# A fused RWKV attention and cosine feed-forward kernel: chunks taken in the order of time over all four batches, with a new hand-written first order

## The chip, the cores and the metric

The kernel runs on one core of a Trainium2 chip. The metric is the device time of one execution in microseconds (us), the median of several runs. Five engines work beside each other: TensorE (PE, its weight loads shown as PEld), VectorE (DVE), ScalarE (ACT), GpSimd (POOL), and SyncE (SP), which here only issues transfers. Each engine runs its own list of instructions in order; semaphores tie the lists together.

## The reference

For each batch and head a 48x48 state runs along 768 steps; the output of all heads is then put through a feed-forward layer with the gate h·cos(h).

```python
batch, n_heads, seq, head_dim = (4, 8, 768, 48)
for t in range(S):
    cur = einsum('bhd,bhe->bhde', u * k[t], v[t])
    y[:, :, t] = einsum('bhd,bhde->bhe', r[t], state + cur)
    state = w[t][..., None] * state + einsum('bhd,bhe->bhde', k[t], v[t])
x = y.transpose(0, 2, 1, 3).reshape(3072, 384)
h = x @ w_in                      # 384 x 2048
out = (h * cos(h)) @ w_out        # 2048 x 384
```

## The kernel before

The time axis is cut into chunks of C=128 steps, so there are 6 chunks for each of 4 batches, 24 in all. Two chunks are worked on together as one **block** (`BLK`=2, i.e. 256 rows of x), so there are 12 blocks. Block i holds chunks number 2i and 2i+1 of the list `order`. Before the change the list takes batches 0 and 1 from their first to their last chunk and then batches 2 and 3: blocks 0 to 5 are a chain through the state of the first two batches, blocks 6 to 11 one through that of the others.

The attention of chunk j is cut into steps, each a short function. `load` fetches the tile `tt` with r, k and w transposed. `decay` (DVE) makes the running products of w by two scans (L207, L213) with `wholes` and a reciprocal (L211, L212) between them, and scales r (L217) and k (L218, on POOL at first) in place. `diag` makes the diagonal of the score matrix: for the first six chunks with PE (`rkt` L204 on DVE, `pc` L224 on PE, `cd` on ACT), later with DVE from a second layout `rk` (L229, L230, L232); POOL spreads it into `asb` (L236). `a` makes the scores (`pa` L259) and copies them into `asb` (DVE, L261). `t` turns k (`pt` L268, copied to `kn`), `d` scales the old state (`dd` L249, copied into `past`). Steps of a whole block are `s` (new state, `pst` L286, `sn` L291/L293), `o` (own part of the output, `py` L314/L319) and `p` (part from the past state, L329/L333, then `xT`: a high part by ACT and a low part by DVE, L144). Chunks with c=0 have no past state: no `d`, and a `p` without matmuls.

The feed-forward of a block is 8 **units** of 256 hidden columns. `mm1` of a unit is 18 matmuls into one PSUM bank `ph` (L381). The **gate** follows: ACT (L357), DVE (L358), ACT sine (L359), DVE product (L360, which also frees the bank), ACT high part `gs` (L141), two POOL low parts (L144). `mm2` is 12 matmuls (L397) into two accumulator banks. All weights stay in SBUF, but each of the 16 slices must be made first from a packed form `raw`: three ACT passes (L163, L166, L167), DVE L168, L169, an ACT cast, and a DVE difference (`w<-h,w`, L144). `raw` slots are a ring of five (`RING`), so a `raw` load waits for ACT's L167 of the slice five before it.

The order in which PE and SP take the first part is written out by hand in `START` (words as `a2` = scores of chunk 2; `f` = fetch a slice, `w` = make one); `PAIR` says for which of blocks 0 and 1 each of the first 16 units is. After that `PLAN` repeats eight slots per block. PE keeps the written order; in the first part SP's transfers keep it too. DVE, ACT and POOL are ordered by the framework's scheduler. A step that isn't there yet when it's needed is called in by `att()` with its `NEEDS` and the rules on buffers. PSUM has eight banks: three for attention (a0 to a2), three for `ph` (h0 to h2), two accumulators; while blocks 0 and 1 run side by side a2 and h2 serve as block 1's accumulators, and attention and `ph` have two banks each.

Of the kernel before, what the change touches and what calls it, by code (L numbers as in the profile page):

```python
# [26 lines left out]
NCB = 6  # L27
W129 = NP * 129
BLK = 2
# [4 lines left out]
RING = 5  # L34
BY_HAND = "P"
MERGE = 1
BUFS = dict(tt=4, rk=2, v=4, h=2, rd=1, rr=7, gs=2, asb=4, ahl=2, sn=2, past=2, xT=2, kn=2, ee=2, dd=2, cd=1, rkt=1)
LEAST = 1e-15
W_SCALE = 2.0 ** 8
INV2PI = 1.0 / (2.0 * math.pi)  # L40
BANKS = dict(a=("a0", "a1", "a2"), h=("h0", "h1", "h2"))
PAIR_W = 2 * HD + 16
VW = NP * PAIR_W
PASSES = ((0, 0), (0, 1), (1, 0))
# [13 lines left out]
        "mm1 mm2",  # L58
        "mm1 mm2",
        "mm1 d+4 d+5 mm2 decay+5 lr+6"]  # L60
START = ["lv0 decay0 diag0 t0 load0 f load1 f d0 a0 f f diag1 w t1 decay2 o0 w a1 f diag2 d1 x0 f load3 p0 f",
# [4 lines left out]
PAIR = "0001100111101010"  # L66
NEEDS = dict(decay="load", lr="load", lv="load", diag="lr", d="decay", a="decay diag", t="decay",
             o="a lv", s="t d lv", p="o d")

# [2 lines left out]
def rwkv_cos_ffn(ctx: ExitStack, tc: tile.TileContext, tr, tn, tv, u, ut, wts, w, rkw, vst, us, xs, out):  # L72
# [15 lines left out]

    def bank(kind, shape, name):

        tags = dict(a=("a0", "a1"), h=("h0", "h1")) if paired[0] else BANKS
        turn[kind] += 1
        return ps.tile(shape, F32, tag=tags[kind][turn[kind] % len(tags[kind])], name=name)

    paired = [True]

    def buf(tag, shape, dtype, name=None, pool=sb):
        return pool.tile(shape, dtype, tag=tag, name=name or tag, bufs=BUFS.get(tag, 1))
    ident = cst.tile([C, C], F32, name="ident")
# [22 lines left out]
    past = [cst.tile([R, NP, R96], F32, name="past%d" % n) for n in range(BLK)]  # L122
# [49 lines left out]
            low_part("wlo%d" % kind, rest, hf, high)  # L172

    NB = NG // NCB
    order = [(b0 + bb) * NCB + c for b0 in range(0, NB, BLK) for c in range(NCB) for bb in range(BLK)]
    atts, states, outs, xts, units, accs = {}, {}, {}, {}, {}, {}

    def att_load(j):
        a = atts[j] = {"j": j}
        a["g"] = g = order[j]  # L180
        a["b"], a["c"] = divmod(g, NCB)
        a["tt"] = tt = buf("tt", [R, TRW], F32)
        for cols in ((1024, TRW), (512, 1024), (0, 512)) if j < IN_PARTS else ((0, TRW),):
            E["qt"].dma_start(out=tt[:, slice(*cols)], in_=tr[g, :, slice(*cols)])
        a["r3"] = tt[:, 0:512].rearrange("p (a t) -> p a t", a=NP)
        a["k3"] = tt[:, 512:1024].rearrange("p (a t) -> p a t", a=NP)
        if j == 0:
            E["qt"].dma_start(out=u_by_head, in_=ut)
        if j == BY_PE:
            E["qt"].dma_start(out=u_sb, in_=u.to_broadcast([C, DM]))  # L190
# [178 lines left out]
    def mm1(t):  # L369
        i, u = seq[t]  # L370
        weights("f", (u + 1) * FU + LEAD + FLEAD)
        weights("w", (u + 1) * FU + LEAD)
        for j in range(BLK):
            att(i * BLK + j, "x")
        xT = xts[i]
        ph = bank("h", [C, FU, BT], "ph")
        for fi in range(FU):
            n = 0
            for kt in range(KT):
                for a, b in PASSES:  # L380
                    nc.tensor.matmul(out=ph[:, fi], lhsT=wgt[u * FU + fi][:, 0, a, kt * 128:(kt + 1) * 128], rhs=xT[:, b, kt],  # L381
                                     start=n == 0, stop=n == 3 * KT - 1)
                    n += 1
        units[t] = gate(sb, ph)

    def mm2(t):
        i, u = seq[t]
        if u == 0:
            tags = ("a2", "h2") if i == 1 else ("acc0", "acc1")
            accs[i] = [ps.tile([C, 512], F32, tag=x, name="acc") for x in tags]  # L390
        gs = units.pop(t)
        todo = [(a, b, fi, j) for a, b in PASSES for fi in range(FU) for j in range(BLK)]
        at_end = i == NBLK - 1 and u == NU - 1
        if at_end:
            todo.sort(key=lambda x: x[3])
        for a, b, fi, j in todo:
            nc.tensor.matmul(out=accs[i][j][:, :DM], lhsT=gs[:, a, fi, j * C:(j + 1) * C],  # L397
                             rhs=wgt[u * FU + fi][:, 1, b],
                             start=u == 0 and fi == 0 and a == 0 and b == 0, stop=u == NU - 1 and fi == FU - 1 and a == 1)
        if u == NU - 1:  # L400
            if i == 1:
                paired[0] = False
            for j in range(BLK):
                ob = buf("rr", [C, DM], F32, "ob")
                with tc.high_priority(offset=HP):
                    if at_end and j:
                        nc.vector.tensor_scalar(out=ob[:, :DM // 2], in0=accs[i][j][:, :DM // 2], scalar1=1.0 / W_SCALE ** 2, scalar2=None, op0=ALU.mult)  # L407
                        nc.scalar.activation(ob[:, DM // 2:], accs[i][j][:, DM // 2:DM], AF.Copy, scale=1.0 / W_SCALE ** 2)  # L408
                    else:
                        nc.scalar.activation(ob, accs[i][j][:, :DM], AF.Copy, scale=1.0 / W_SCALE ** 2)  # L410
                chunk = order[i * BLK + j]
                if at_end and j:
                    nc.sync.dma_start(out=out[chunk * C:(chunk + 1) * C, :DM // 2], in_=ob[:, :DM // 2])
                    nc.scalar.dma_start(out=out[chunk * C:(chunk + 1) * C, DM // 2:], in_=ob[:, DM // 2:])
                else:
                    E["qo"].dma_start(out=out[chunk * C:(chunk + 1) * C, :], in_=ob)
# [4 lines left out]
    seq, at_unit = [], [0, 0]  # L421
    for i in PAIR:
        seq.append((int(i), at_unit[int(i)]))
# [7 lines left out]
                 a=att_scores, t=att_transpose, s=att_state, o=att_own, p=att_past, x=att_x)  # L431

    def att(j, n):

        whole = n in "osp"
        if not 0 <= j < (NBLK if whole else NG) or (j, n) in seen:
            return
        for m in ("decay" if n == "diag" and j < BY_PE else NEEDS.get(n, "")).split():
            for c in (range(j * BLK, (j + 1) * BLK) if whole and m not in "osp" else (j,)):
                att(c, m)  # L440
        i = j // BLK
        if n == "load":
            for m in "osp":
                att((j - BUFS["tt"]) // BLK, m)
        elif n == "t" or n == "d":
            att(i - 1, "s")
        elif n == "lv":
            att((j - BUFS["v"]) // BLK, "o")
            att((j - BUFS["v"]) // BLK, "s")
        elif n == "x":  # L450
            att(i, "p")
        elif n == "p":
            att(j - 1, "s")
        seen.add((j, n))
        if n == "load":
            att_load(j)
        else:
            steps[n](j if whole else atts[j])
# [8 lines left out]
    def up(n):  # L467

        if n == 0 and up1[0] < slots:
            if up1[0] - up1[1] > LAG:  # L470
                up(1)
            mm1(up1[0])
            up1[0] += 1
        elif n == 1 and up1[1] < up1[0]:
            mm2(up1[1])
            up1[1] += 1

    def events(i, row, t=None):
        for e in row.split():
            if e == "mm1":  # L480
                if t is not None:
                    up(0)
            elif e == "mm2":
                if t is not None and up1[1] <= t - LAG:
                    up(1)
            else:
                n, _, d = e.partition("+")
                att(i * (1 if n in "osp" else BLK) + int(d), n)
# [26 lines left out]
    with tc.manual_schedule(engines={dict(P=ET.PE, S=ET.SP)[e] for e in BY_HAND}):  # L515
        for row in START:
            for e in row.split():
                if e in ("mm1", "mm2"):
                    up(int(e[-1]) - 1)
                elif e in ("f", "w"):  # L520
                    weights(e, done[e] + 1)
                else:
                    att(int(e[-1]), e[:-1])
# [173 lines left out]
```

## Time and profile before

| | before |
|---|---|
| median of 3 runs (lowest, highest) | 562.46 us (560.8, 562.49) |
| the profiled execution, its own time | 563.24 us |
| its span, first to last instruction | 561.2 us |
| PE busy | 521.7 us, 93% |
| DVE busy | 368.5 us, 66% |
| ACT, POOL busy | 271.4 us, 239.3 us |
| mean granted TensorE clock | 0.980 of full speed |

The span is 2.0 us shorter than the profiled execution's own time; what lies around it isn't in the trace. A busy share is a mean over stages; what limits is read stage by stage.

### The profile page before, as it was taken

Reading aid. Unit: us, or ns where it says so; the run is one execution under the profiler, and the core shown is the slowest. Engines: PE = TensorE matmul, PEld = TensorE weight load, DVE = VectorE, ACT = ScalarE, POOL = GpSimd, SP = SyncE. Lnnn points to the kernel's source line nnn. Section 1 sums busy time; section 2 is a strip of 40 time slices with the busy share of each in tenths; the row PEclk is TensorE's granted clock in tenths of the full one; section 3 lists DMA queues with packets and bytes.
Section 4 is the critical chain, followed back from the end, with each engine's and each line's share of the span. In section 5 each row is a group of like instructions: output and inputs, shape, how many; then the busy total and the mean of one; then the engine's idle time right before and its main releaser. Section 6 shows DMA issues by size and latency. Waiting matters only on the chain. (4 is left out here: it accounts for less than half of the span.)

```text
span 561.2 us, 11935 instructions
## 1 busy us (share of the span) xinstructions
PE 521.7 (93%) x4964; PEld 493.4 (88%) x4964; DVE 368.5 (66%) x556; ACT 271.4 (48%) x454; POOL 239.3 (43%) x290
## 2 busy tenths in 40 slices
PE   2676888999999999999999999999999999999996
PEld 2575887999899999999999998998999999999996
DVE  5899999956959559548478458458548448633331
ACT  2677998844443433543454334434444444444542
POOL 3241347444445445436436336435436333313332
PEclk9986898999999999999999999999999999999999
DMA  8983870115242043051331060051041036000000
GB/s 244 310 260 122 288 218 1 57 30 168 79 113 77 15 118 87 29 148 42 91 100 29 29 166 24 29 149 40 29 118 44 29 115 225 25 8 1 29 2 30
DMA packets 16728, 52.17 MB, mean 93 GB/s; under 512 B 2016, under 2 KB 8416, under 8 KB 16672
## 3 DMA queue, kind: packets, MB, share of 16 engines
q1 hardware_dynamic: 16528, 51.28, 30.7%
q8 instruction: 40, 0.66, 0.5%
q14 instruction: 16, 0.13, 0.1%
q10 hardware_dynamic: 144, 0.10, 0.1%
HBM read 46.65 MB, written 4.72 MB: 92 GB/s over the span
## 5 line engine op out<-in xcount | busy, mean ns | idle before, releaser
L144 POOL TENSOR_TENSOR gs<-rr,gs 128x256 fp32r<-128x256 f32 x192 | 161.3, 861 | 205.0 <-ACT gs L141 177.0
L397 PE MATMUL acc<-w,gs 128*128 128x384 f32 x1152 | 223.3, 342 | 5.7 <-POOL gs L144 3.6
L381 PE MATMUL ph<-xT,w 128*128 128x256 f32 x1728 | 223.7, 284 | 4.8 <-DVE rr L360 4.8
L381 PEld LDWEIGHTS ph<-xT,w 128*128 128x128 f32 x1728 | 215.2, 190 | 8.5 <-issue 3.0
L397 PEld LDWEIGHTS acc<-w,gs 128*128 128x128 f32 x1152 | 197.6, 188 | 13.0 <-POOL gs L144 7.3
L359 ACT ACTIVATE rr<-rr,quarter 128x512 f32<-128x512 f32 x96 | 69.4, 723 | 117.5 <-DVE rr L358 117.5
L358 DVE SCALAR_TENSOR_TENSOR rr<-rr,ph 128x512 f32<-128x512 int32 x96 | 65.4, 681 | 75.6 <-ACT rr L357 62.8
L360 DVE TENSOR_TENSOR rr<-rr,ph 128x512 f32<-128x512 f32 x96 | 65.5, 682 | 43.7 <-ACT rr L359 43.3
L357 ACT ACTIVATE rr<-ph 128x512 int32<-128x512 f32 x96 | 57.0, 594 | 59.1 <-PE ph L381 58.4
L141 ACT CAST gs<-rr 128x512 fp32r<-128x512 f32 x96 | 58.8, 613 | 49.3 <-PE acc L397 44.1
L236 POOL TENSOR_SCALAR_AFFINE_SELECT asb<-cd 128x512 f32<-128x512 f32 x48 | 32.0, 691 | 40.1 <-PE py L319 26.6
L207 DVE TENSOR_TENSOR_SCAN ee<-tt,one_e 112x516 f32<-112x516 f32 x24 | 35.0, 1458 | 15.3 <-DMA tt<-tr 14.9
L259 PE MATMUL pa<-tt 48*128 48x128 f32 x384 | 33.8, 305 | 10.0 <-DVE tt L217 5.4
L259 PEld LDWEIGHTS pa<-tt 48*128 48x128 f32 x384 | 28.0, 204 | 16.2 <-POOL gs L144 5.6
L261 DVE COPY_PREDICATED asb<-mask,pa 128x512 f32<-128x512 uint8 x48 | 33.0, 735 | 4.1 <-PE pa L259 3.9
L217 POOL TENSOR_TENSOR tt<-tt 112x512 f32<-112x512 f32 x18 | 25.9, 1441 | 22.3 <-DVE tt L213 21.2
L213 DVE TENSOR_TENSOR_SCAN tt<-tt,inj 112x516 f32<-112x516 f32 x24 | 31.3, 1306 | 0.2
L229 DVE TENSOR_TENSOR rk<-rk 128x384 f32<-128x384 f32 x18 | 15.2, 844 | 21.2 <-DMA rk<-tn 21.1
L141 ACT COPY past<-dd 48x192 f32<-48x192 f32 x40 | 14.0, 350 | 21.3 <-POOL dd L249 20.6
L218 POOL TENSOR_TENSOR tt<-tt,ee 112x512 f32<-112x512 f32 x6 | 10.1, 1683 | 28.2 <-DVE rkt L204 10.8
L224 PE MATMUL pc<-u_by_head,rkt 112*128 112x2 f32 x48 | 7.7, 282 | 12.1 <-DVE rkt L204 7.6
L224 PEld LDWEIGHTS pc<-u_by_head,rkt 112*128 112x128 f32 x48 | 7.5, 237 | 12.9 <-DVE rkt L204 7.6
(68 smaller groups left out, 371.2 us busy)
## 6 DMA issues: line engine op xcount, KB each, us to landing
tt<-tr SPq DMA_DIRECT2D x22, 674.2 KB, 7.1
raw<-wts SPq DMA_DIRECT2D x16, 768.0 KB, 8.7
rk<-tn SPq DMA_DIRECT2D x18, 384.0 KB, 3.9
v<-tv SPq DMA_DIRECT2D x24, 224.0 KB, 6.2
ww<-w SPq DMA_DIRECT2D x6, 768.0 KB, 4.5
out<-ob SPq DMA_DIRECT2D x23, 192.0 KB, 2.0
tt<-tr SPq DMA_DIRECT2D x4, 224.0 KB, 6.7
tt<-tr SPq DMA_DIRECT2D x2, 226.2 KB, 6.1
```

The lines of the kernel that those rows point to most:

```text
L141: (nc.scalar.copy if E[name] is nc.scalar else E[name].tensor_copy)(out=out, in_=in_)
L144: E[name].tensor_tensor(out=out, in0=full, in1=high.bitcast(F32), op=ALU.subtract)
L207: nc.vector.tensor_tensor_scan(out=ee.rearrange("p a t -> p (a t)")[:, ::-1], data0=wp[:, 1:W129 + 1][:, ::-1], data1=one_e.rearrange("p a ...
L236: nc.gpsimd.affine_select(out=asb, in_=col.unsqueeze(2).to_broadcast([C, NP, C]), pattern=[[0, 4], [1, C]], compare_op=ALU.is_equal, fill= ...
L259: nc.tensor.matmul(out=pa[h][:, p], lhsT=a["k3"][rows(h), p], rhs=a["r3"][rows(h), p], start=True, stop=True)
L261: nc.vector.copy_predicated(a["asb", h], mask, pa[h])
L357: nc.scalar.activation(nn, ph, AF.Copy, scale=INV2PI / W_SCALE, bias=0.25)
L358: nc.vector.scalar_tensor_tensor(out=rr, in0=nn, scalar=-2.0 * math.pi * W_SCALE, in1=ph, op0=ALU.mult, op1=ALU.add)
L359: nc.scalar.activation(rr, rr, AF.Sin, scale=1.0 / W_SCALE, bias=quarter)
L360: nc.vector.tensor_tensor(out=rr, in0=rr, in1=ph, op=ALU.mult)
L381: nc.tensor.matmul(out=ph[:, fi], lhsT=wgt[u * FU + fi][:, 0, a, kt * 128:(kt + 1) * 128], rhs=xT[:, b, kt], start=n == 0, stop=n == 3 * K ...
L397: nc.tensor.matmul(out=accs[i][j][:, :DM], lhsT=gs[:, a, fi, j * C:(j + 1) * C], rhs=wgt[u * FU + fi][:, 1, b], start=u == 0 and fi == 0 a ...
```

## The change

1. `order` goes by time: chunk c of batches 0, 1, 2, 3, then chunk c+1. Blocks 0 and 1 both hold first chunks (c=0), and block i depends on the state of block i-2 (`SAME` = 2).
2. `START` and `PAIR` are new. Scores and outputs of blocks 0 and 1 come ahead of any transposition or state, and the first three units are block 0's.
3. Banks by stage: attention may also use the two accumulator banks until block 0's first `mm2`; from then three and three, two and two while block 1's accumulators live in a2 and h2, then three and three.
4. Buffers: `rd` 2 instead of 1, `sn`, `kn`, `dd` 4 instead of 2; and the rules in `att()` that go with the new order.

```diff
-BUFS = dict(tt=4, rk=2, v=4, h=2, rd=1, rr=7, gs=2, asb=4, ahl=2, sn=2, past=2, xT=2, kn=2, ee=2, dd=2, cd=1, rkt=1)
+BUFS = dict(tt=4, rk=2, v=4, h=2, rd=2, rr=7, gs=2, asb=4, sn=4, xT=2, kn=4, ee=2, dd=4, cd=1, rkt=1)
-BANKS = dict(a=("a0", "a1", "a2"), h=("h0", "h1", "h2"))
+BANKS = dict(a=("a0", "a1", "a2", "acc0", "acc1"), h=("h0", "h1", "h2")), dict(a=("a0", "a1"), h=("h0", "h1")), dict(a=("a0", "a1", "a2"), h=("h0", "h1", "h2"))
-START = ["lv0 decay0 diag0 t0 load0 f load1 f d0 a0 f f diag1 w t1 decay2 o0 w a1 f diag2 d1 x0 f load3 p0 f",
...
+START = ["load0 load1 f lv0 decay0 f diag0 a0 lv1 decay1 diag1 a1 w load2 f w o0 mm1",
+         "load3 f lv2 w decay2 w f mm1 diag2 a2 lv3 decay3 mm2 w w f diag3 a3 mm1 o1 f",
+         "mm1 w f t0 t1 s0 load4 mm2 mm1 w f lv4 mm2 mm1 w f load5 lv5 mm2 mm1 w f t2 t3 s1",
...
-PAIR = "0001100111101010"
+PAIR = "0001110101010101"
-        tags = dict(a=("a0", "a1"), h=("h0", "h1")) if paired[0] else BANKS
+        tags = BANKS[stage[0]]
-    order = [(b0 + bb) * NCB + c for b0 in range(0, NB, BLK) for c in range(NCB) for bb in range(BLK)]
+    order = [b * NCB + c for c in range(NCB) for b in range(NB)]
+    SAME = NB // BLK
+            if i < 2:
+                stage[0] = 1 if i else 2
-        elif n == "t" or n == "d":
-            att(i - 1, "s")
+        elif n == "t":
+            att((j - BUFS["kn"]) // BLK, "s")
+        elif n == "d":
+            att(i - SAME, "s")
+            att((j - BUFS["dd"]) // BLK, "s")
+            att(i - 1, "p")
-        elif n == "p":
-            att(j - 1, "s")
```

The lists hold the same instructions, but for two `dd` that go from DVE to POOL (DVE has 4 before and 2 now, POOL 16 and 18). Line numbers of the changed file stand 1 to 5 higher. Three places of the lists show what moves.

PE, from the first matmul of the program; before, then the change (`pc` diagonal, `pa` scores, `py` own output, `pt` transposition, `ph` is mm1):

```order
L224 MATMUL pc<-u_by_head,rkt 128x2 x4
L268 MATMUL pt<-ident,tt 128x112 x4
L259 MATMUL pa<-tt 128x128 x8
L224 MATMUL pc<-u_by_head,rkt 128x2 x4
L268 MATMUL pt<-ident,tt 128x112 x4
L259 MATMUL pa<-tt 128x128 x8
L314 MATMUL py<-asb,v 32x128 x8
```

```order
L225 MATMUL pc<-u_by_head,rkt 128x2 x4
L260 MATMUL pa<-tt 128x128 x8
L225 MATMUL pc<-u_by_head,rkt 128x2 x4
L260 MATMUL pa<-tt 128x128 x8
L315 MATMUL py<-asb,v 32x128 x8
L320 MATMUL py<-asb,v 32x128 x8
L315 MATMUL py<-asb,v 32x128 x8
L320 MATMUL py<-asb,v 32x128 x8
L382 MATMUL ph<-xT,w_181 128x256 x9
```

Transpositions and states leave this place; the first unit follows block 0's own output at once, where before the state of block 0 and a third chunk's diagonal stand between.

DVE, the change alone, from just behind block 1's `xT` on (`w_...<-h,w` ends the making of a weight slice, `rr` is a gate, `rkt` the first work on chunk 4, `sn` block 0's new state):

```order
L144 TENSOR_TENSOR xT<-py,xT 128x384 x2
L168 TENSOR_SCALAR h<-h 128x768
L144 TENSOR_TENSOR w_618<-h,w_618 128x2x384
L169 ISA h<-h,rd 128x1536
L230 TENSOR_TENSOR rk<-rk 128x384
L168 TENSOR_SCALAR h<-h 128x768
L359 SCALAR_TENSOR_TENSOR rr<-rr,ph 128x512
L231 TENSOR_TENSOR rk<-rk,u_sb 128x384
L292 COPY sn<-pst 112x192 x2
L361 TENSOR_TENSOR rr<-rr,ph 128x512
L144 TENSOR_TENSOR w_672<-h,w_672 128x2x384
```

Before, block 0's two `sn` stand ahead of the first gate on DVE; now they stand inside the fourth gate, and all weights from the ninth slice on come behind them.

SP, the transfers of the first part; before, then the change (`raw` is a packed weight slice, `tt` a chunk, x3 or 512 columns is a chunk fetched in parts):

```order
L184 DMA tt<-tr 112x517
L184 DMA tt<-tr 112x512 x2
L188 DMA u_by_head<-ut 112x8
L198 DMA v<-tv 128x448
L151 DMA raw<-wts 128x1536
L184 DMA tt<-tr 112x517
L184 DMA tt<-tr 112x512 x2
...
L198 DMA v<-tv 128x448 x2
L151 DMA raw<-wts 128x1536
L184 DMA tt<-tr 112x1541
```

```order
L185 DMA tt<-tr 112x517
L185 DMA tt<-tr 112x512 x2
L189 DMA u_by_head<-ut 112x8
L185 DMA tt<-tr 112x517
L185 DMA tt<-tr 112x512 x2
...
L151 DMA raw<-wts 128x1536 x8
L191 DMA u_sb<-u 128x384
L195 DMA rk<-tn 128x768 x2
L151 DMA raw<-wts 128x1536
L185 DMA tt<-tr 112x1541
```

Chunk 1 now goes ahead of the first weights. The last `tt` of each piece is chunk 4: before it stands behind 9 `raw` loads, now behind 14.

## Rows read from the trace of the kernel before

**Rows 1.** The page: busy tenths of PE and DVE in 40 slices of 14.0 us.

```profile
PE   2676888999999999999999999999999999999996
...
DVE  5899999956959559548478458458548448633331
```

**Rows 2.** Stages: window and its length, then busy us (and instructions) of PE, PEld, DVE, ACT and POOL, granted clock, DMA share, GB/s.

```profile
42.00:56.00 14.00, 8.62 (x136) 7.17 (x137) 13.32 (x19) 10.41 (x16) 2.50 (x3) 0.63 0.39 121
...
98.00:112.00 14.00, 14.00 (x108) 13.40 (x106) 14.00 (x22) 11.39 (x17) 6.74 (x6) 1.00 0.17 57
...
0.00:117.00 117.00, 86.56 (x734) 79.42 (x735) 105.31 (x153) 85.68 (x124) 47.93 (x50) 0.91 0.60 180
...
0.00:68.63 68.63, 42.99 (x429) 37.52 (x430) 58.73 (x88) 45.13 (x65) 21.14 (x27) 0.88 0.80 244
...
117.00:160.00 43.00, 41.77 (x480) 39.21 (x479) 30.46 (x47) 18.66 (x34) 21.05 (x27) 1.00 0.30 90
160.00:540.00 380.00, 376.94 (x3648) 358.98 (x3647) 228.09 (x350) 160.37 (x285) 164.64 (x206) 1.00 0.24 71
```

**Rows 3.** Whom PE waited for: us in total, times, longest. The first row is of the first 115 us, the second of 160 to 540 us.

```profile
PE ph L381 <- DVE rr L360: 4.8, 5, 1.9
...
PE acc L397 <- POOL gs L144: 2.9, 6, 0.9
```

**Rows 4.** PE in order of time: start, us, what, and in brackets the idle time ahead of it. The first row is the first mm1, the last two are the 13th and 14th.

```profile
35.47 3.18 PE L381 MATMUL ph<-xT,w 128*128 128x256 f32 x18
...
53.48 1.02 PE L329 MATMUL py<-tt,past 112*32 112x128 f32 x16
...
55.03 2.39 PE L381 MATMUL ph<-xT,w 128*128 128x256 f32 x18
...
78.55 0.95 PE L224 MATMUL pc<-u_by_head,rkt 112*128 112x2 f32 x8
...
99.67 0.55 PE L268 MATMUL pt<-ident,tt 112*128 112x112 f32 x4
...
102.25 1.16 PE L259 MATMUL pa<-tt 48*128 48x128 f32 x16
...
112.78 2.37 PE L381 MATMUL ph<-xT,w 128*128 128x256 f32 x18 [0.68 <-DVE rr L360]
...
117.07 2.29 PE L381 MATMUL ph<-xT,w 128*128 128x256 f32 x18
```

**Rows 5.** DVE in order of time, same columns. The fourth row ends the making of the ninth weight slice, the fifth is the last operation of the 12th gate.

```profile
4.03 1.23 DVE L207 TENSOR_TENSOR_SCAN ee<-tt,one_e 112x516 f32<-112x516 f32 x1 [1.97 <-DMA tt<-tr]
...
12.74 1.23 DVE L207 TENSOR_TENSOR_SCAN ee<-tt,one_e 112x516 f32<-112x516 f32 x1 [3.15 <-DMA tt<-tr]
...
39.96 1.97 DVE L211 TENSOR_SCALAR wholes<-ee 112x4 f32<-112x4 f32 x1
...
67.69 0.94 DVE L144 TENSOR_TENSOR w<-h,w 128x768 fp32r<-128x768 f32 x1
...
115.53 0.69 DVE L360 TENSOR_TENSOR rr<-rr,ph 128x512 f32<-128x512 f32 x1 [0.79 <-ACT rr L359]
```

**Rows 6.** DVE's instructions of the first 117 us grouped by form: busy us, mean ns | idle ahead of them.

```profile
L213 DVE TENSOR_TENSOR_SCAN tt<-tt,inj 112x516 f32<-112x516 f32 x8 | 10.3, 1293 | 0.1
...
L261 DVE COPY_PREDICATED asb<-mask,pa 128x512 f32<-128x512 uint8 x10 | 6.8, 720 | 0.6 <-PE pa L259 0.5
...
L211 DVE TENSOR_SCALAR wholes<-ee 112x4 f32<-112x4 f32 x8 | 5.2, 649 | 0.0
...
L212 DVE RECIPROCAL inj<-wholes 112x4 f32<-112x4 f32 x8 | 1.4, 172 | 0.1
L249 DVE TENSOR_TENSOR dd<-sn,ee 112x192 f32<-112x192 f32 x4 | 1.4, 341 | 0.0
L218 DVE TENSOR_TENSOR tt<-tt,ee 112x512 f32<-112x512 f32 x2 | 1.3, 668 | 0.0
...
L230 DVE TENSOR_TENSOR rk<-rk,u_sb 128x384 f32<-128x384 f32 x2 | 1.1, 540 | 0.0
```

**Rows 7.** What DVE would wait for: on ACT the last two passes over weight slice 0, the table load ahead of the first sine, and the copies to `kn` of the first 117 us (grouped); on POOL a k scaling, a pair of spreads and the first gate's low parts; and POOL's `dd` (min/median/max ns).

```profile
12.51 1.06 ACT L166 ACTIVATE rd<-raw 128x768 int16<-128x768 uint32 x1
13.43 1.04 ACT L167 ACTIVATE rd<-raw 128x768 f16<-128x768 f32 x1
...
41.24 1.28 ACT L359 ACT_TABLE_LOAD   x1
...
L141 ACT COPY kn<-pt 128x384 f32<-128x384 f32 x5 | 2.3, 470 | 1.5 <-PE pt L268 1.4
...
39.55 1.19 POOL L218 TENSOR_TENSOR tt<-tt,ee 112x512 f32<-112x512 f32 x1 [4.33 <-DVE ee L207]
40.69 1.22 POOL L236 TENSOR_SCALAR_AFFINE_SELECT asb<-cd 128x512 f32<-128x512 f32 x2
45.37 1.85 POOL L144 TENSOR_TENSOR gs<-rr,gs 128x256 fp32r<-128x256 f32 x2 [3.45 <-ACT gs L141]
...
L249 POOL TENSOR_TENSOR dd<-sn,ee x16: 511/516/827, 138.7 to 462.1; 112x192 f32<-112x192 f32 x16
```

**Rows 8.** SP's issue of `raw` 13 (of 0 to 15), and the time to landing of the four `tt` loads issued between 30 and 117 us.

```profile
64.96 0.33 SPq L151 DMA_DIRECT2D raw<-wts  x1
...
DMA to landing us min/median/max: 6.7/8.7/10.8
```

More of the change, by code (lines that the diff above doesn't have):

```diff
@@ L89, in bank @@
     def bank(kind, shape, name):
-        tags = dict(a=("a0", "a1"), h=("h0", "h1")) if paired[0] else BANKS
+        tags = BANKS[stage[0]]
         turn[kind] += 1
         return ps.tile(shape, F32, tag=tags[kind][turn[kind] % len(tags[kind])], name=name)
-    paired = [True]
+    stage = [0]
     def buf(tag, shape, dtype, name=None, pool=sb):
@@ L401, in mm2 @@
             if i == 1:
-                paired[0] = False
+                stage[0] = 2
             for j in range(BLK):
```

6 rows, old and new, of the table START are left out of this document.

## Prediction, made before the changed kernel was run

> **What bounds the kernel now.** I read the slices of the page first [rows 1]: PE has nine tenths or more from the eighth slice to the last, while in the first 100 us or so it does not, and there DVE stands at nine tenths. The stages say it in numbers [rows 2]: from 98 to 112 us both engines have no gap; to 117 us PE is idle 117 - 86.6 = 30.4 us and DVE only 11.7; from 160 to 540 us PE is idle 3.1 of 380 us and DVE busy 60%. So there are two regimes: a start in which DVE (weights, decays, gates) sets the pace, and a long part at PE's pace. Whom PE waited for [rows 3] shows in the second regime 2.9 us, on POOL. In the first it names among others DVE's L360 five times: an mm1 can't start until the gate two units back has freed its bank. The last such wait stands ahead of the 13th mm1 at 112.78; the 14th at 117.07 has none [rows 4], since its gate, the 12th, ended on DVE at 115.53 + 0.69 = 116.22 [rows 5], 0.85 us earlier. From there on PE's remaining work alone sets the end. The question is thus when DVE hands over the gates up to the 12th, and how much PE work is then left.
>
> **The change part by part.** All engines do the same work, two `dd` apart, so nothing is gained or lost but waits.
>
> *DVE's work ahead of the 12th gate.* Both lists have all 16 weight slices there. Against before, the new list has one scan, one `wholes`, one reciprocal, one k scaling (L218), one `rk` product (L230) and two `dd` less, and two score copies (L261) more; `sn` are four in both. With the mean durations [rows 6]: 1.29 + 0.65 + 0.17 + 0.67 + 0.54 + 2 x 0.34 - 2 x 0.72 = 2.6 us less. A `wholes` alone is 0.17 when POOL leaves it be, and a mean holds 0.08 of overlap, so I take **2.4 less** (bounds 2.0 and 2.6).
>
> *PE's work ahead of the 14th mm1.* Both orders have 13 mm1, 10 mm2, two own outputs and two states there. The new one has a diagonal (0.95) and a chunk's scores (half of 1.16) more, a transposition (0.55) and a past part (53.48 to 55.03, 1.55) less [rows 4]: 0.6 us less is done by then, so that much more is left. At full clock the past part is shorter; I take **0.5 lost** (0.2 to 0.6).
>
> *The slack.* Before, the 12th gate came 0.85 us before its mm1 could run. In the new order the PE work ahead is smaller and the gate, by what follows, decides: **0.8 gained**.
>
> *DVE's idle time up to that gate.* Before it is 11.7 us to 117 [rows 2], some 0.4 of them behind the gate: 11.3. Along the new lists I find these waits:
> - The first scan waits as before, 1.0 for the program's start and 1.97 for `tt` [rows 5]: 3.0. The second one waited 3.15 for chunk 1, which stood behind `v` and a weight slice; now it goes ahead of them, lands while DVE is on chunk 0, and this wait goes.
> - What is late next: weight slice 0, behind 690 - 229 KB more. DVE reaches it at some 14 us and waits for ACT's two passes (1.06 and 1.04 [rows 7]): 1.1. The first `xT` waits for the own output: 0.7. The first gate's product waits for the sine and its table load (1.28): 1.2. Chunk 3's score copy waits for POOL, where the spread stands behind the second gate's low parts (1.85): 1.8. `sn`, now inside the fourth gate, waits for mm1, two transpositions, two `kn` copies (0.47 each) and the state: 1.4. Small ones: 0.3, and the 12th gate's sine, 0.8 as now.
>
> Without the first 3.0 and the last 0.8 these are 6.5, walked with unhindered durations. Where DVE is itself held up, what it would wait for gets ready meanwhile; I take half, 3.3 (bounds 1 and 6.5). The clock: in 42 to 56 us the granted clock is 0.63, the mean of its two levels, 1.2 and 2.4 GHz, after stretches in which PE had little to do [rows 2]; the first mm1 took 3.18 where later ones take 2.29 [rows 4]. The new order puts three units and two score steps into a like stretch, in the chain that feeds DVE: 1.5 (0 to 3).
>
> *Chunk 4's load.* Tiles `tt` are four; before, chunk 0's was read by its transposition among PE's first instructions. Now that comes behind block 1's first mm1, and on SP the load stands behind `raw` 13, which waits for ACT's passes on slice 8. `raw` 13 went out at 64.96 [rows 8]. DVE's work up to the ninth slice's end was 58.73 us, the end was 68.63 [rows 2, 5]; in the new list it comes 2.7 us of work earlier and with less idle time ahead, so `raw` 13 goes at about 59.5, and the transposition is over at about 60. With 6.7 to 10.8 us to landing [rows 8] chunk 4 is there at 66.8 to 70.9. DVE needs it for `rkt`, 58.4 us of work into its list (the same number of instructions as up to 68.63 but one) and 7.3 of idle time: 65.7. So DVE waits 1.1 to 5.2; the load has little else to share the queue with, and I take 2.0. This is a new wait, and everything on DVE is queued behind it: weights 10 to 16, gates, decays.
>
> Sum: 3.0 + 3.3 + 1.5 + 2.0 + 0.8 = 10.6 against 11.3: **0.7 gained**.
>
> *POOL and the shared way to SBUF.* A `wholes` of 0.17 took 1.97 at 39.96 while POOL ran a scaling and spreads (39.55 to 41.91) [rows 5, 7]. The means above hold such hindrance. POOL has as many gates as before ahead of the 12th (10 to 11), and one pair of spreads (1.22) and two `dd` (0.52 each) more [rows 7]: 2.3 us; at before's ratio, (0.65 - 0.17) x 8 = 3.8 us of `wholes` on 47.9 us of POOL, that is 0.2, which I leave out. The Trainium skill (SBUF — State Buffer, Who interferes with whom) says that a DVE and a POOL instruction that both need the shared ports exclude each other for a whole instruction, so earlier POOL work can cost DVE its full length; the trace agrees for that one row, and by the rule the 2.3 would all be lost.
>
> *The rest.* `rd` and the other buffers take no time; two banks more at the start and three for `ph` in the first units free waits that the trace hardly has (`pa`, `pc` wait for DVE's data there). After 160 us the lists agree but for POOL's `dd`, which now stands between the two k scalings, 0.52 each in some seven blocks: nothing, where POOL idles there; 3.6 us if it all reached the mm2 that waits for POOL. I take 0.
>
> Total: 2.4 - 0.5 + 0.8 + 0.7 = **3.4 us faster**. The profiled execution took 563.24 and would take 559.8; that execution is 0.8 above the median, 562.46, from which I forecast **559.1 us**.
>
> **The rivals.**
> 1. *No change.* The chain waits aren't covered: 6.5 instead of 3.3 leaves a gain of 0.2, 562.3 us. Or the `dd` on POOL costs its 3.6: 562.7. For it: DVE has nearly the same work in the same stretch, and is the limiter. Against: the 3.15 is surely gone. Chance 0.22.
> 2. *Slower, by chunk 4's load.* If slice 8 is no earlier on ACT, `raw` 13 goes at 64.96, and with 8.7 us to landing chunk 4 is there at 74.0: DVE waits 8.3 instead of 2.0, and 3.4 - 6.3 is a loss of 2.9: 565.4. It eats the gain from a landing at 71.1 on, and makes the kernel measurably slower from 72.8 on. For it: the buffers come free much later than before, and DVE has no reserve. Against: block 0's gates and `rd` let ACT run ahead. Chance 0.18.
> 3. *POOL excludes DVE* for the whole 2.3 us: 3.4 - 2.3 = 1.1 gained, 561.4. One row speaks for it, the means against. Chance 0.05.
> 4. *More gained.* Nearly all waits are covered and chunk 4 lands in time: 5.0 idle instead of 10.6, and of PE's 43 - 41.8 = 1.2 idle after 117 us [rows 2] 0.5 goes as gates run ahead: 3.4 + 5.6 + 0.5 = 9.5 gained, 553.0. Chance 0.13.
>
> **How the numbers follow.** The forecast has 0.42, with a range of its own from 556.5 to 560.8 (idle 8 to 12.3). A measurement of this kernel tells about 0.3% (1.7 us) from no change: under 560.8 is faster, above 564.1 slower. Faster: forecast, rival 4 and a part of rival 3, some 0.58; within: 0.24; slower: 0.18. The range from 554.0 to 565.5 leaves out about half of rivals 2 and 4. Both signs are in it.
>
> **What would show it.** Right: DVE's second scan starts near 8 us without a wait; the first mm1 near 25 us (35.5 before); the 12th gate on DVE at 113 to 114, its mm1 just behind; PE idle to then some 3 us less. The `rkt` of chunk 4 with a wait for `tt` of about 2. Wrong: that wait at 5 or more (rival 2); waits of DVE for `pst`, `pa` or sines above 6 in sum (1); new waits of PE for POOL after 160 us (1); longer means of DVE's forms (3).

## The result, and the profile after

The changed kernel took 569.84 us (median of 4 runs) where the kernel before took 562.48 beside it: a ratio of 1.0123, 95% interval 1.0082 to 1.0164. Timed once more (run e0), it was 568.64 against 562.09, 1.0121 (1.0082 to 1.0161). It is slower by some 7 us, where 3.4 faster was forecast. One of the four, the profiled one, took 643.43 us at a granted clock of 0.75; the median counts it, the ratio does not, and all rows "of after" are those of e0, whose span is 567.7 us at 0.97.

The stages of after, columns as in [rows 2], which answer to [rows 1] too; the last one is a piece of the second:

```profile
0.00:117.00 117.00, 90.47 (x722) 83.65 (x723) 106.23 (x152) 83.52 (x120) 50.83 (x53) 0.88 0.55 180
117.00:160.00 43.00, 38.41 (x416) 36.44 (x418) 27.84 (x45) 17.48 (x33) 19.02 (x24) 0.92 0.30 90
160.00:540.00 380.00, 373.97 (x3681) 353.98 (x3672) 233.49 (x348) 159.27 (x286) 164.22 (x204) 1.00 0.24 71
131.00:144.00 13.00, 9.45 (x76) 8.99 (x75) 7.42 (x15) 3.79 (x7) 1.92 (x3) 0.74 0.53 143
```

Up to 117 us PE is busy 3.9 us longer than before, at a clock of 0.88 instead of 0.91. From 117 to 160 us it is idle 4.6 us instead of 1.2, and the clock is 0.92 instead of 1.00; from 160 to 540 it is idle 6.0 us instead of 3.1 [rows 2]. The loss thus lies where the forecast saw nothing but work. PE in order of time, to set beside [rows 4]: the first mm1, the 14th, the end of `START` with its wait, and the first own output (L315, step `o`) of block 3 and of block 11:

```profile
22.92 1.12 PE L382 MATMUL ph<-xT,w 128*128 128x256 f32 x4
...
115.07 2.37 PE L382 MATMUL ph<-xT,w 128*128 128x256 f32 x18 [0.44 <-DVE rr L361]
...
135.47 1.94 PE L287 MATMUL pst<-v,kn 128*64 128x48 f32 x32 [3.55 <-ACT kn L141]
137.35 1.83 PE L269 MATMUL pt<-ident,tt 112*128 112x112 f32 x8
138.86 3.81 PE L382 MATMUL ph<-xT,w 128*128 128x256 f32 x18
...
158.93 0.65 PE L315 MATMUL py<-asb,v 128*32 128x128 f32 x16
...
500.36 0.64 PE L315 MATMUL py<-asb,v 128*32 128x128 f32 x16
```

The same two own outputs of before:

```profile
157.43 0.64 PE L314 MATMUL py<-asb,v 128*32 128x128 f32 x16
...
493.35 0.64 PE L314 MATMUL py<-asb,v 128*32 128x128 f32 x16
```

These are the same place in both programs, so they cut the loss in three: after is 2.0 us ahead at the 14th mm1 and 1.5 behind at block 3's own output, loses another 5.5 in the eight blocks that follow (341.4 against 335.9 us), and gains 0.5 in the rest (67.3 against 67.9). I call the time from one block's own output to the next's an *interval*. It holds that block's past part and state and the next one's transpositions. Read off the starts of these rows:

| kernel | block 3's `o` at | the eight intervals, us | sum |
|---|---|---|---|
| before | 157.43 | 42.69, 41.39, 41.04, 40.48, 43.25, 43.55, 42.37, 41.15 | 335.9 |
| after (e0) | 158.93 | 43.43, 43.09, 43.03, 43.99, 42.78, 43.13, 42.09, 39.89 | 341.4 |
| e9, order of pairs | 158.42 | 42.54, 41.49, 40.67, 40.48, 43.16, 41.96, 42.28, 41.11 | 333.7 |
| e11, mixed order | 157.79 | 42.72, 42.80, 41.59, 40.63, 43.34, 42.94, 41.73, 41.11 | 336.9 |
| e12, after, r scaled by DVE | 158.86 | 42.02, 41.66, 41.72, 43.12, 41.74, 41.74, 41.14, 39.89 | 333.0 |
| e14, before, r scaled by DVE | 156.27 | 41.88, 40.92, 41.33, 40.48, 42.74, 42.13, 41.77, 41.11 | 332.4 |

A block is *light* where a step falls out: the last chunks have no transposition and no state (blocks 5 and 11 before, 10 and 11 after), the first chunks no past part (blocks 0 and 6 before, 0 and 1 after). So before, the second to fourth intervals and the eighth lack a step; after, the last two do, and the first six are all full.

### The profile page after: what moved, and what is told of

It reads as the page before. It is cut to its first block, busy times and chain, and to the rows that moved or that the text cites. A ratio compares the mean times of both kernels' runs of the same rounds, so it can differ in the third digit from the quotient of the medians.

```text
span 641.7 us, 11914 instructions
## 1 busy us (share of the span) xinstructions
PE 613.2 (96%) x4964; PEld 563.5 (88%) x4964; DVE 379.5 (59%) x554; ACT 273.7 (43%) x454; POOL 243.7 (38%) x292
## 5 line engine op out<-in xcount | busy, mean ns | idle before, releaser
L382 PE MATMUL ph<-xT,w 128*128 128x256 f32 x1728 | 266.0, 316 | 10.1 <-ACT w L141 3.8
L382 PEld LDWEIGHTS ph<-xT,w 128*128 128x128 f32 x1728 | 254.9, 215 | 17.5 <-ACT w L141 4.6
L400 PE MATMUL acc<-w,gs 128*128 128x384 f32 x1152 | 263.5, 386 | 0.0
L144 POOL TENSOR_TENSOR gs<-rr,gs 128x256 fp32r<-128x256 f32 x192 | 156.1, 835 | 250.3 <-ACT gs L141 235.8
L400 PEld LDWEIGHTS acc<-w,gs 128*128 128x128 f32 x1152 | 219.9, 200 | 20.8 <-ACT rr L360 2.0
L359 DVE SCALAR_TENSOR_TENSOR rr<-rr,ph 128x512 f32<-128x512 int32 x96 | 65.3, 680 | 117.5 <-ACT rr L358 103.3
L218 POOL TENSOR_TENSOR tt<-tt 112x512 f32<-112x512 f32 x18 | 28.9, 1605 | 19.2 <-DVE tt L214 16.8
L250 POOL TENSOR_TENSOR dd<-sn,ee 112x192 f32<-112x192 f32 x18 | 14.5, 804 | 45.6 <-DVE ee L208 45.6
L230 DVE TENSOR_TENSOR rk<-rk 128x384 f32<-128x384 f32 x18 | 12.8, 710 | 20.3 <-DMA rk<-tn 20.3
L231 DVE TENSOR_TENSOR rk<-rk,u_sb 128x384 f32<-128x384 f32 x18 | 20.9, 1162 | 0.3
L315 PE MATMUL py<-asb,v 128*32 128x128 f32 x384 | 19.9, 321 | 0.6 <-DVE asb L262 0.5
L320 PE MATMUL py<-asb,v 128*32 128x128 f32 x384 | 19.7, 325 | 0.0
```

What stands on the lines that cost most here:

```text
L144: E[name].tensor_tensor(out=out, in0=full, in1=high.bitcast(F32), op=ALU.subtract)
L359: nc.vector.scalar_tensor_tensor(out=rr, in0=nn, scalar=-2.0 * math.pi * W_SCALE, in1=ph, op0=ALU.mult, op1=ALU.add)
```

## Experiments

**The three runs that came first (e0, e1, e2).** e0 is the changed kernel itself. e1 keeps the order of time and its rules and buffers, with `START`, `PAIR` and banks of before. e2 takes only the new banks away (code cut at the dots):

```
- BANKS = dict(a=(... 5 banks ...), ...), ...      # e2: stage 0 gets two and two
+ BANKS = dict(a=("a0", "a1"), h=("h0", "h1")), ...
-                 stage[0] = 1 if i else 2
+                 stage[0] = 1
```

> Time order with its rules and the new buffer counts, but the first order, the pairing of units and the banks of before. If the time order itself costs in the long part (B): 566 to 572 us. If the new first order is what costs (A): 560 to 564 us, like before; below 560 if the time order helps by itself.

> The changed kernel with the banks of before: two for the scores and two for mm1 until block 1's accumulators are free. If the new banks matter in the first units (they allow three mm1 ahead): slower than the changed kernel by 1 us or more, 570.5 to 574. If they are beside the point, because units wait for weights and xT there: 568 to 570.

e1: 575.22 us, ratio 1.0254 (1.0224 to 1.0283). e2: 568.72, 1.0116 (1.0078 to 1.0153). By the medians the new opening, with its pairs and banks, is worth some 6.6 us to the order of time (e1's executions go from 570.13 to 577.02), the banks nothing, and the order of time costs in either opening.

**The end of the opening (e3, e4, e7).** In after, the copy to `kn` for which PE waits 3.55 us stands on ACT behind two sines that wait for DVE:

```profile
131.74 0.72 ACT L360 ACTIVATE rr<-rr,quarter 128x512 f32<-128x512 f32 x1 [4.12 <-DVE rr L359]
...
133.82 0.72 ACT L360 ACTIVATE rr<-rr,quarter 128x512 f32<-128x512 f32 x1 [0.87 <-DVE rr L359]
134.44 0.60 ACT L141 CAST gs<-rr 128x512 fp32r<-128x512 f32 x1
134.95 0.85 ACT L141 COPY kn<-pt 128x384 f32<-128x384 f32 x2
```

After this gap the granted clock is at its lower level for a time (0.74 over the 13 us above, 0.53 from 135.4 to 142.5), and the mm1 at 138.86 takes 3.81 us where others take 2.29. I moved the transpositions away from the state:

```
- "mm2 mm1 o2 p2 mm2 mm1 lv6 load7 mm2 x4 x5 mm1 mm2 t4 t5 s2"     after
+ "mm2 mm1 t4 t5 mm2 o2 p2 mm1 lv6 load7 mm2 x4 x5 mm1 mm2 s2"     e3 (e4: s1 also behind one more mm1)
+ "mm2 mm1 o2 p2 mm2 mm1 lv6 load7 t4 t5 mm2 s2 x4 x5 mm1 mm2"     e7
```

> The transpositions of chunks 4 and 5 (t4, t5) are put three groups of products ahead of the scores of their pair (s2), where the changed kernel has the three back to back at the end of its opening order. Theory A (the loss between 117 and 165 us is PE waiting 3.5 us at s2 for ScalarE's copy of kn, and the half clock that follows): the wait for kn near 135 us falls under 1 us, the half clock near 136 to 143 us goes, and the time is 562 to 565.5 us. Rival B (PE would have waited at that place for something else, the loads of rk or the sines among it, so that the wait only moves): PE's idle time from 117 to 160 us stays within 1 us of the 4.8 us of the changed kernel and the time stays at 567.5 to 569.5 us. Rival C (the steady blocks carry the whole loss): also 567.5 to 569.5 us, with the idle time of the stretch less by 2 us or more.

> As the kernel with t4 and t5 early, and the scores of chunks 2 and 3 (s1) also put behind one more first product, where they stood right behind t2 and t3. Theory A: the wait of 2.2 us at s1 near 80 us and the half clock that follows it at 82 to 88 us go as well, which is up to 2.2 us of wait and 3 us of clock, so 558 to 563 us. If the stretch up to 117 us is set by DVE and not by PE's order, the clock comes back but DVE's work ends no sooner: then the same as with t4 and t5 alone, within 1 us.

> t4 and t5, the group of second products, and s2 now come one pair of product groups earlier than in the changed kernel, with a group between the transpositions and s2 and another between s2 and the next transpositions; in DVE's order the sums sn then still stand ahead of the two scans of chunks 8 and 9, which they do not where t4 and t5 were moved alone. Theory A2 (the kn copy and the sn sums at the end of the opening order cost PE its 3.5 us and the half clock, and in the run with t4 and t5 early the 6.0 us wait came from sn behind those scans): PE is idle under 1.7 us from 117 to 160 us, its clock there stays at 1.0, and the time is 561.5 to 565 us. Rival B2 (DVE's loads of rk and of tt set this stretch, whatever PE's order): idle 4 us or more again, at another place, and 567.5 to 570 us.

All were slower still: e3 572.55 us, ratio 1.0190 (1.0134 to 1.0246); e4 574.73, 1.0216 (1.0147 to 1.0285); e7 575.28, 1.0205 (1.0169 to 1.0240). The wait for `kn` went and one of 6 us came at another place. e3, PE and then DVE, then e7, PE and DVE:

```profile
139.67 0.98 PE L269 MATMUL pt<-ident,tt 112*128 112x112 f32 x4 [5.99 <-issue]
...
132.24 1.22 DVE L208 TENSOR_TENSOR_SCAN ee<-tt,one_e 112x516 f32<-112x516 f32 x1
...
138.95 0.62 DVE L294 TENSOR_TENSOR sn<-pst,dd 112x192 f32<-112x192 f32 x2
```

```profile
131.47 1.76 PE L269 MATMUL pt<-ident,tt 112*128 112x112 f32 x8 [5.99 <-DVE xT L144]
...
127.71 0.56 DVE L230 TENSOR_TENSOR rk<-rk 128x384 f32<-128x384 f32 x1 [1.25 <-DMA rk<-tn]
...
130.87 1.01 DVE L144 TENSOR_TENSOR xT<-py,xT 128x384 fp32r<-128x384 f32 x2
```

Until block 1 is done attention has two banks of kind `a`. In e3 the trace names no releaser, but the second transposition starts as soon as DVE's `sn` has read `pst` (139.57), and `sn` now stands behind the scans of two chunks; in e7 it starts just as DVE's `xT` reads `py`, and `xT` stands behind products of `rk` that wait for their loads. A and A2 fell: in both runs PE waits there for work that stands in DVE's queue, and moving the PE step only moved the wait. e10, below, has e7's wait once more (5.8 us). In e4 the other move costs too: block 2's own output starts at 122.97, against 120.28 in e3.

**POOL's `dd`, and earlier loads (e5, e6, e8, e10).** e5 gives `dd` to DVE after the opening (the text below says from the fourth chunk; it is from chunk 6), e6 is e4 and e5 together. e8 sets the past part ahead of the mm2 in `PLAN`, and e10 is e7 and e8:

```
- LATER = dict(... dd="p", ...)                 # e5
+ LATER = dict(... dd="v", ...)
- PLAN: "mm1 o+1 mm2 diag+5 p+1 lv+6 ..."       # e8
+ PLAN: "mm1 o+1 p+1 mm2 diag+5 lv+6 ..."
```

> From the fourth chunk on the sum dd is made by DVE and no longer by POOL; the order of PE is that of the changed kernel. Theory D (dd now stands between POOL's two scalings of k and delays the gate's cast for PE, 5.5 us in 12 waits after 117 us against 3.6 us in 7 before): PE's wait for POOL at acc falls to 3 us or less and the time is 565 to 567 us. Rival E (those waits come from DVE's late tt, on which POOL's second scaling waited 2.0 us): DVE with 8 to 16 more additions is later still, and the time is 568.5 to 571 us.

> From block 2 on the products with the past state stand ahead of the group of second products that they stood behind, so tt's buffers come free and the next two tt loads start some 2.2 us sooner; the opening is that of the changed kernel. Theory F (the stalls after 160 us begin with DVE waiting 2.3 us per block for those loads, which puts scans, gates and POOL's second scaling late): DVE's wait for tt falls from 11.5 us in 7 to under 3 us, PE's waits for POOL from 5.5 us in 12 to 3 us or less, and the time is 565 to 567.5 us. Rival H (DVE's and POOL's work in that stretch is too much in any order): PE's waits stay at 4.5 to 6 us and the time at 568 to 570 us.

e5: 568.61 us, 1.0114 (1.0062 to 1.0167); PE's waits for POOL after 160 us are 4.8 us in 12. So it isn't `dd`. e6 took 573.57, against 555 to 561 if all had added; e10 573.12, against 558.5 to 562.5. e8: 569.38, 1.0117 (1.0098 to 1.0135). There DVE's waits for `tt` fall from 11.5 us to 1.9, as theory F wants, and PE's waits for POOL are gone, but a gate's L359 now stands behind the scans and their followers, and the sine waits for it. PE's waits in e8 from 160 to 540 us, and ACT at one such place:

```profile
PE acc L400 <- ACT gs L141: 8.6, 7, 1.5
PE ph L382 <- DVE inj L213: 1.0, 2, 0.6
...
310.46 0.72 ACT L360 ACTIVATE rr<-rr,quarter 128x512 f32<-128x512 f32 x1 [5.90 <-DVE rr L359]
```

So F had the waits right and the time wrong. In e5 and e8 the loss stays (568.61 and 569.38 against 568.64), and in e8 PE waits 8.6 us for ACT where it had waited 5.5 for POOL.

**The order alone (e9, e13, e11).** e9 is after with the chunks in the order of before; e13 has the old opening too, so that only rules, buffers and banks are new; e11 takes the first chunks of all batches and then two batches to their end, with a buffer of its own for each batch's state (not in the cut):

```
- order = [b * NCB + c for c in range(NCB) for b in range(NB)];  SAME = NB // BLK
+ order = [(b0 + bb) * NCB + c for b0 ... for c in range(NCB) for bb ...];  SAME = 1    # e9, e13
+ order = [b * NCB for b in range(NB)] + [... for c in range(1, NCB) ...];  SAME = 1    # e11
- "... diag3 a3 mm1 o1 f", "mm1 w f t0 t1 s0 load4 ..."
+ "... diag3 a3 mm1 t0 t1 s0 d2 d3 o1 p1 f", "mm1 w f load4 ..."                        # e9
```

> The changed kernel with its chunks in the order of before (two batches to their end), and in the new opening order t0, t1, s0 and the decayed states of chunks 2 and 3 put forward, since these chunks follow chunks 0 and 1 there. Theory G (the order of time makes all steady blocks full ones, where the order of before has two light ones in the middle: no t and s for the last chunks of two batches, no past for the first of the next two): PE's waits for POOL after 160 us are 3 to 4 us in 6 to 8 waits, and if the end of the opening costs what it does in the changed kernel the time is 564 to 566.5 us. Rival I (the loss after 160 us belongs to something else that changed with it, buffers or banks): the waits stay near 5.5 us in 12 and the time is 567.5 us or more.

> The first chunks of all four batches as in the changed kernel, whose opening order stands unedited, then two batches to their end and the other two after them, so that one light block (the last chunks of two batches, without t and s) lies in the middle again; each batch's state has a buffer of its own. Theory G (the loss after 160 us goes by the number of full blocks in a row: a full block took 43.0 us from its o to the next in the changed kernel, a light one 40.5 to 41.5 us in both others): the eight intervals between the o groups add up to 337.5 to 340.5 us, between the 333.7 us of the order of pairs and the 341.4 us of the order of time, and the time is 564.5 to 567.5 us. Rival J (what costs is that four batches' states are alive at once and a state is two blocks old): that holds here for two batches only and from block 3 on no state but those is used, so 333.5 to 336 us for the intervals and 561 to 563.5 us.

> The changed kernel's rules, buffers and banks with the order of chunks, the opening order and the pairs of before: the fourth corner beside before's own buffers. If the buffers and rules carry the 2.2 us that the intervals of the kernel with the new opening and the old order were shorter by than those of before (333.7 against 335.9 us): 559 to 561 us, faster than before by 0.2 to 0.6 per cent. If those 2.2 us come from the new opening order: 561.5 to 563.5 us.

e9: 561.38 us, ratio 0.9991 (0.9966 to 1.0016): undoing the order alone, with the steps of `START` that then have to come sooner, takes the whole loss away, more than theory G asked. PE's waits in it from 160 us on, against 5.5 us in 12 of after:

```profile
PE acc L400 <- POOL gs L144: 1.3, 3, 0.5
PE acc L400 <- DVE rr L359: 0.3, 1, 0.3
```

e13: 562.97, 0.9991 (0.9963 to 1.0018), block 3's `o` at 158.19 where e9 has 158.42. So in the order of pairs the new opening is worth nothing that can be measured, nor are the buffers. The eight intervals of e13 add up to 334.8 us, halfway between before and e9, so what shortens those of e9 stays open.

e11: 563.60, 1.0001 (0.9978 to 1.0024), with 336.9 us of intervals. That lies between the two expectations: above J's 336, below G's 337.5, and the time is nearer to J's. By the table, before's four full intervals are 43.0 on the mean and after's six 43.2: there the number of full blocks gives most of the 5.5 us, as G says. e11's five full ones are 42.7, which is 2.7 of the 4.6 us that its intervals are shorter than after's. So G gives less than half of that; why these blocks are shorter stays open, and rival J is not ruled out for it.

**What a full block loses its time to (e12, e14, e15, e16).** POOL, in a full block of after, then PE and DVE at the same place:

```profile
303.40 2.35 POOL L144 TENSOR_TENSOR gs<-rr,gs 128x256 fp32r<-128x256 f32 x2 [1.33 <-ACT gs L141]
305.71 2.11 POOL L218 TENSOR_TENSOR tt<-tt 112x512 f32<-112x512 f32 x1
307.78 1.04 POOL L250 TENSOR_TENSOR dd<-sn,ee 112x192 f32<-112x192 f32 x1
310.80 1.19 POOL L218 TENSOR_TENSOR tt<-tt 112x512 f32<-112x512 f32 x1 [1.98 <-DVE tt L214]
311.94 1.73 POOL L144 TENSOR_TENSOR gs<-rr,gs 128x256 fp32r<-128x256 f32 x2
...
312.72 0.62 PE L400 MATMUL acc<-w,gs 128*128 128x384 f32 x2 [0.69 <-POOL gs L144]
313.73 0.62 PE L400 MATMUL acc<-w,gs 128*128 128x384 f32 x2 [0.39 <-POOL gs L144]
...
303.45 1.77 DVE L214 TENSOR_TENSOR_SCAN tt<-tt,inj 112x516 f32<-112x516 f32 x1
305.14 1.70 DVE L208 TENSOR_TENSOR_SCAN ee<-tt,one_e 112x516 f32<-112x516 f32 x1
```

POOL's second scaling (L218; it is r's, the prediction wrongly wrote k) waits 2 us for DVE's scan, and the low parts that PE needs are queued behind it. A full block of before reads the same, and PE waits there twice for POOL, 0.59 and 0.39 us. Before's light block has low parts between the scalings, and PE waits for nothing:

```profile
341.25 1.71 POOL L217 TENSOR_TENSOR tt<-tt 112x512 f32<-112x512 f32 x1
344.60 1.19 POOL L217 TENSOR_TENSOR tt<-tt 112x512 f32<-112x512 f32 x1 [1.64 <-DVE tt L213]
345.74 1.73 POOL L144 TENSOR_TENSOR gs<-rr,gs 128x256 fp32r<-128x256 f32 x2
```

```profile
295.12 1.19 POOL L217 TENSOR_TENSOR tt<-tt 112x512 f32<-112x512 f32 x1 [4.56 <-DVE tt L213]
296.26 2.36 POOL L144 TENSOR_TENSOR gs<-rr,gs 128x256 fp32r<-128x256 f32 x2
300.68 1.19 POOL L217 TENSOR_TENSOR tt<-tt 112x512 f32<-112x512 f32 x1 [2.06 <-DVE tt L213]
302.58 1.58 POOL L144 TENSOR_TENSOR gs<-rr,gs 128x256 fp32r<-128x256 f32 x2 [0.72 <-ACT gs L141]
```

So I took the scaling off POOL from chunk 6 on (the first text below again says the fourth), in after (e12), before (e14), e9 (e15) and e11 (e16):

```
- LATER = dict(... r3="p", k3="v", ...)
+ LATER = dict(... r3="v", k3="v", ...)
```

> The changed kernel with DVE doing the second scaling (r by pp) from the fourth chunk on, which POOL did. Theory K (a full block loses its 1 to 2 us because POOL's queue holds the gates' cast behind a scaling that waits for DVE's scan, and POOL's scaling slows the scans that run beside it, 1.7 us against 1.2): PE's waits for POOL after 160 us fall under 2 us, the eight intervals add up to 338 us or less, and the time is 563.5 to 566.5 us. Rival L (DVE's own work between two gates is what is too long, and this edit adds 1.4 us to it in each block): the waits turn into waits for ScalarE's cast of gs, the intervals stay at 341 to 345 us, and the time is 568 to 573 us.

> The kernel before with the scaling of r done by DVE and not by POOL after the opening, nothing else. If POOL's scalings ahead of the gates' cast cost a full block 1 to 2 us in either order of chunks, the four full blocks of before give back 3 to 4.5 us: the eight intervals between the o groups go from 335.9 to 331.5 to 333 us, and the time to 558 to 560 us. If the loss belongs to the order of time alone, the intervals stay at 335 us or more and the time within 1 us of before.

> The order of pairs with the new opening and the new buffers (561.4 us), and the scaling of r on DVE. Its intervals hold some 3.7 us of waits (333.7 us against 330 us without one): if they go, 558 to 559.5 us; if the new opening then ends later because DVE has two scalings more before 120 us, 559.5 to 561.5 us.

> The order with all four first chunks ahead and then two batches to their end (563.6 us), and the scaling of r on DVE. Its intervals add up to 336.9 us; without waits 331 to 332 us: 558 to 560 us. The 3.6 us for which PE waits for kn at the end of the opening stays, since nothing of the edit touches it.

PE's waits from 160 us on in e12, and in e14:

```profile
PE acc L400 <- POOL gs L144: 0.9, 1, 0.9
```

```profile
PE acc L397 <- POOL gs L144: 1.1, 2, 0.7
```

e12: 564.57 us, 1.0022 (0.9993 to 1.0050), with 333.0 us of intervals, 8.4 less than after with the same PE program; 5.1 of them are PE's idle time (6.0 to 1.0), the rest is a quicker mm2. The six full intervals fall by 1.2 on the mean, the last, light one stays at 39.89. Theory K holds, and DVE had room for the 1.4 us a block. Its executions spread from 561.3, the profiled one, to 566.7, the longest at the lowest granted clocks (0.964 and 0.965), so that the medians differ by 4.1 only.

e14: 557.96, 0.9920 (0.9885 to 0.9955): the kernel before loses time to the same queue, its intervals go from 335.9 to 332.4 us, and this version beats both kernels. e15: 559.79, 0.9964 (0.9937 to 0.9991), with 331.5 us of intervals and an opening that ends 0.9 us later than e9's. e16: 559.84, 0.9942 (0.9912 to 0.9972), with 333.8. So without that scaling on POOL the eight intervals of the profiled executions come to 331.5 to 333.8 us in every order, where with it they went from 333.7 to 341.4.

The medians say less. e14 gains 4.4 us over before and e12 4.1 over after, so the order of time costs 1.2% against the kernel before with the scaling on POOL (1.0121) and still 1.0% without it (1.0022 against 0.9920). With the new opening on both sides it costs 1.3% with it (after and e9) and 0.6% without (e12 and e15). The profiled execution of e12 is its fastest; what its others lose, and where, is in no trace. So the scaling is shown as the cause for the intervals that were profiled; of the whole loss it is about half by the second comparison and less by the first. Why e12 stands 4.7 us above e16, which has its opening and a like wait for `kn`, stays open but for a piece: at the end of the opening PE waits 2.6 us in e12 for a copy of an output on ACT (`ob`), and 1.3 in e16. What moves the clock from one execution to the next wasn't tried.

## Why the prediction was wrong

- *The start, to the 12th gate: right in kind, too large.* The second scan starts at 7.99 without a wait, the first mm1 at 22.92 (25 forecast). The gate's last product starts at 114.23 and ends at 114.92, 1.3 us earlier than before; 3.1 were forecast.
- *PE's work ahead of the 14th mm1, 0.5 lost: misread.* The 16 matmuls of 1.16 us are the scores of one chunk, not of two: before has 384 for 24 chunks. With 1.16 in place of its half the two orders do the same work by then, to 0.01 us, and nothing is lost.

```profile
L259 PE MATMUL pa<-tt 48*128 48x128 f32 x384 | 33.8, 305 | 10.0 <-DVE tt L217 5.4
```

- *DVE's idle time: right in its sum, by luck in its parts.* To the gate DVE was busy 104.15 us (106.23 less 2.08 behind it) and so idle 10.8, against 11.3: 0.5 gained, 0.7 forecast. `raw` 13 went out at 59.46 (59.5 forecast), but chunk 4's `rkt` waited 0.45 us for its load (2.0), and the `rkt` waited 1.7 us for PE's `pc`, which the forecast had not listed:

```profile
L205 DVE TENSOR_TENSOR rkt<-tt 112x512 f32<-112x512 f32 x6 | 4.2, 706 | 2.2 <-PE pc L225 1.7 <-DMA tt<-tr 0.4
```

- *DVE's work, 2.4 less: mis-sized.* Before it was 104.9 to the gate, so 0.75 less. The counts were right, the means were not. The add of the weights, grouped, before and then after:

```profile
L169 DVE CUSTOM_DVE_ANT_0 h<-h,rd 128x1536 uint16<-128x1536 uint16 x16 | 15.1, 941 | 0.9 <-ACT rd L167 0.8
```

```profile
L169 DVE CUSTOM_DVE_ANT_0 h<-h,rd 128x1536 uint16<-128x1536 uint16 x16 | 18.4, 1147 | 0.3
```

  That is 3.3 us more for the same 16. The first of them, beside POOL's work of that time:

```profile
14.58 2.88 DVE L169 CUSTOM_DVE_ANT_0 h<-h,rd 128x1536 uint16<-128x1536 uint16 x1
...
12.96 2.51 POOL L219 TENSOR_TENSOR tt<-tt,ee 112x512 f32<-112x512 f32 x1 [1.75 <-DVE rkt L205]
15.43 1.22 POOL L237 TENSOR_SCALAR_AFFINE_SELECT asb<-cd 128x512 f32<-128x512 f32 x2
```

  It ends 0.8 us after POOL's spreads do, having taken 2.88 where 0.94 is usual. This is rival 3's mechanism, which I had at 0.05 and 2.3 us; other work grew shorter, so a net 1.65 of the term is gone. The Trainium skill (SBUF — State Buffer, Who interferes with whom) has a DVE and a POOL instruction that both need the shared ports exclude each other for a whole instruction; the 2.88 us of this row agree.
- *"From there on PE's remaining work alone sets the end": the step that failed.* It took the waits after 117 us as a constant of the kernel, 1.2 and 3.1 us. The first goes by the order of steps at the end of `START`, the second by the kinds of blocks that follow. The 2.0 us of lead at the 14th mm1 became a lag of 1.5 at block 3's own output. There PE was idle 3.4 us more (4.6 against 1.2), the half clock cost some 3.0 (135.47 to 142.50 are 7.0 us for a state, two transpositions and an mm1, which after 160 us take 1.06, 0.70 and 2.21), and 1.6 less was to do between the two places (a diagonal and a chunk's scores less, a transposition more: 0.95 + 1.16 - 0.55). That gives 4.8, where 3.5 are missing, so this closes to 1.3 us only.
- *"After 160 us ... I take 0": the other half.* I compared the lists and found `dd` moved; e5 shows that `dd` isn't it. What I didn't ask is which blocks stand there. The order of time moves the past-less block 1 into the opening, where DVE sets the pace and PE's saving buys nothing, and with it 1.2 us of PE work (163.09 to 164.26 for a past part) into the intervals. It also makes six full blocks in a row. With 5.5 us lost in the intervals, 4.3 are waits and lesser pace. In the profiled executions POOL's scaling ahead of the low parts makes most of them: without it the two orders' intervals differ by 0.6 us (333.0 in e12, 332.4 in e14). By the medians that is not shown: there e12 and e14 are 6.6 us apart, as after and before are, and what keeps them apart stays open.
- The sign of "new waits of PE for POOL after 160 us" stood under rival 1, for its 3.6 us through `dd`. The sign came, its cause there fell with e5. Rival 2, which had my chance for slower, did not happen, and no rival had the order of the blocks itself.

## What to carry to other kernels

Where a change of order moves the exceptions, the first and last pieces that do less, ask which stretch they leave: a light piece is worth its saving and its missing waits only where the engine it relieves is the bound. A wait of about 1% of a long stretch can hang on one instruction in an in-order queue that waits for another engine ahead of work that the bound engine needs; move that instruction, not the step that waits. Before shifting a step in an opening, look at which queue its data comes through: three times here the wait only changed its name.

## What was not expected of the hardware

One scaling of 112x512 took POOL 1.19 us alone and 2.11 beside a scan of DVE; that scan took 1.70 us, and the one ahead of it, beside POOL's low parts, 1.77, where 1.20 to 1.23 is usual. Both engines lose. And a gap of 3.55 us on PE was followed by products at half clock, 3.81 us instead of 2.29 for the next mm1, which costs about as much as the gap itself.
